# A loop that works out the order of the attention stage, and weights that load in halves

## The chip, the core and the metric

The kernel runs on one core of a Trainium2 chip. The core has five engines with a queue each: TensorE (PE, with its weight loads as PEld), VectorE (DVE), ScalarE (ACT), GpSimd (POOL) and SyncE (SP), which here only issues transfers. Each engine runs its queue in order. The metric is the time of one execution on the device in microseconds, the median of several runs.

## What is computed

Attention over 4 batches and 8 heads, 576 positions, head size 64, with a window of 128 and a slope per head; then a soft mixture of 8 experts on the 2304 rows of 512; then a layer with a squared ReLU.

```python
def _attn_ref(q, k, v):                      # (4, 8, 576, 64)
    scores = scale * q @ k.T
    scores = where((rel >= 0) & (rel < 128), scores + bias, -1e9)
    attn = exp(scores - max); attn /= sum(attn) + 1e-9
    return attn @ v
def _moe_ref(x, phi, w1, w2):                # x (2304, 512), 32 slots
    logits = x @ phi
    d = softmax(logits, axis=0)
    slot_input = (d.T @ x).reshape(8, 4, 512)
    slot_out[e] = maximum(slot_input[e] @ w1[e], 0) @ w2[e]
    return softmax(logits, axis=1) @ slot_out
def _moe2_ref(x, w_in, w_out):
    h = maximum(x @ w_in, 0)
    return h * h @ w_out
```

## The kernel before

The first stage, some 130 us, is attention with the dispatch half of the mixture. Its **units** are pairs of heads of one batch, 16 of them (u), four to a batch. A unit has 9 chunks of 64 rows (c); two chunks make a **step** (t), 72 steps. Of each step, in order of need:

- emit_S: two score products on TensorE (tile s, L166), into one of three PSUM banks "S".
- emit_max: on VectorE, bias added and the row's minimum taken (p, st, L174), into one of NP = 5 buffers p.
- emit_exp on ScalarE (L185), emit_sums on GpSimd (L190), emit_recip on VectorE (L195; for two steps together), emit_norm with emit_fold on GpSimd (L209, L219).
- emit_T: two transposes of p on TensorE (tile tp, L233). They free the buffer p for the step five later.
- emit_evac: the transposed blocks go to the ring ptb, first on ScalarE (L245), then the half blocks on VectorE (L249, L251).

When the steps of a unit are through, emit_PV (L261, tiles xa and xb) makes the product with v, emit_xT (L273, L278) copies it, and emit_xn transposes it back (X, L302; Y, L306) and copies it (xn_all, L307; xnr, L309). After four units come the logits (L, L289, L295) and then d0 to d4, the dispatch of that batch: max and exp of the logits, a transpose of dT (L339), its copy dn on VectorE (L340, L342), the product R with dn (L347, L350) and the sum acc (L357, L359).

**What sets the order.** The loop over t at L436 emits it by hand: scores of step t + 1, transposes of step t - LT (LT = 4), PV of a unit when its time has come, then evacuation, max, sums, exp, reciprocal and norm, and at last what run_side holds for that t (L390 to L419 fill the table). The order in which it is emitted is the order in each engine's queue.

**Transfers.** All go through SyncE's queue. When the scores of a unit's last chunk have been emitted, z and k of the unit two later (three later for the first two) are issued (L448 on; they wait until the buffer is free), and after them one weight tile of 1 MB, at units 4, 7, 10 and 13 two (load_next_w, L65). v of unit u + 2 follows emit_xT of unit u. The weight ring has 19 tiles. As the stage ends, pools close and five extra tiles and yw are loaded into their room. Then the products H (L650) and O (L789) use the weights.

Of the kernel before, what the change touches and what calls it, by code (L numbers as in the profile page):

```python
# [12 lines left out]
ALU = mybir.AluOpType  # L13
# [15 lines left out]
def attn_moe_relu2_kernel(ctx: ExitStack, tc: tile.TileContext, z, k, v, phi, w1, w2, w_in, w_out, bias, cst, out):  # L29
# [130 lines left out]
    def emit_S(t):  # L160
        sb_t[t] = bank("S", "s")
        if t % 2 == 0:
            st_t[t // 2] = apool.tile([128, 12], F32, tag="st", name="st", bufs=4)
# [5 lines left out]
    def emit_max(t):  # L169
        for i in range(2):  # L170
            u, c, n, e = info[2 * t + i]
            p = pbuf[t % NP][:, e:e + n]
            pr = u % NPAIR
            dve.tensor_tensor_reduce(  # L174
                out=p, in0=sb_t[t][:, 256 * i:256 * i + n], in1=tbl[:, 192 * pr + 192 - n:192 * pr + 192],
                scale=-0.125, scalar=3.0e38, op0=ALU.add, op1=ALU.min, accum_out=st_t[t // 2][:, 2 * (t % 2) + i:2 * (t % 2) + i + 1],
            )
        sb_t.pop(t)

    def emit_exp(t):  # L180
        st, k = st_t[t // 2], 2 * (t % 2)
        for i in range(2):
            u, c, n, e = info[2 * t + i]
            p = pbuf[t % NP][:, e:e + n]
            act.activation(out=p, in_=p, func=AF.Exp, bias=st[:, k + i:k + i + 1], scale=-1.0, accum_out=st[:, 4 + k + i:5 + k + i])  # L185
# [25 lines left out]
    def emit_norm(t):  # L211
        st, k = st_t[t // 2], 8 + 2 * (t % 2)
        emit_fold(t)
        for i in range(2):
            u, c, n, e = info[2 * t + i]
            o = e + n - 128 if c % 2 else e
            p = pbuf[t % NP][:, o:o + min(n, 128)]
            eng = dve if t >= NS - 2 and i == 1 else pool
            eng.tensor_scalar(out=p, in0=p, scalar1=st[:, k + i:k + i + 1], scalar2=0.0, op0=ALU.mult, op1=ALU.add)  # L219
# [52 lines left out]
    def emit_xT(u):  # L272
        act.activation(out=xT[u][:, 0:512], in_=xa_t.pop(u), func=AF.Copy)  # L273
        dst = xT[u][:, rem(u // NPAIR)]
# [7 lines left out]
    L_t = {}  # L282
# [14 lines left out]

    def emit_xn(u):
        kk = u % NPAIR
        X = bank("T" if kk == NPAIR - 1 or u == NU - 2 else "B", "X")  # L300
        for g in range(4):
            pe.transpose(X[:, 128 * g:128 * g + 128], xT[u][:, 128 * g:128 * g + 128], ident)  # L302
        sl = slice(128 * kk, 128 * kk + 128)
        if u // NPAIR % 2:
            Y = bank("T", "Y")
            pe.transpose(Y[:, 0:128], xT[u][:, 512:640], ident)  # L306
        dve.tensor_copy(out=xn_all[:, :, sl], in_=X.rearrange("p (g d) -> p g d", g=4))  # L307
        if u // NPAIR % 2:
            act.activation(out=xnr[:, sl], in_=Y[:, 0:128], func=AF.Copy)  # L309
# [26 lines left out]
    def emit_d2(b):  # L336
        X = bank("T", "X")
        for c in range(0, wid(b), 128):
            pe.transpose(X[:, c:c + 128], dT[:, c:c + 128], ident)  # L339
        dve.tensor_copy(out=dn[:, 0:128], in_=X[:, 0:128])  # L340
# [49 lines left out]
    side, side0 = {}, {}  # L390
    last_T = {}
    for u in range(NU):
        t0 = (NCH * u + 8) // 2 + (LT if u < NU - 1 else LT - 1)
        add = lambda dt, f, *a: side.setdefault(t0 + dt, []).append((f, a))
        side0.setdefault(t0 + 1, []).append((u,))
        add(1, emit_xT, u)
        late = u == NU - 1
        if late:
            break
        if u < NU - 2:  # L400
            add(4, emit_xn, u)
        if u % NPAIR == NPAIR - 1:
            for x in range(u - 3, u + 1):
                add(3, emit_logits, x)
            for x in range(u - 3, u + 1):
                add(3, emit_logr, x)
        if u == NU - 2:
            for x in range(u - 2, u + 1):
                add(3, emit_logits, x)
            for x in range(u - 2, u + 1):  # L410
                add(3, emit_logr, x)
        if u % NPAIR == NPAIR - 1:
            b = u // NPAIR
            add(4, emit_d0, b)
            add(5, emit_d1, b)
            add(6, emit_de, b)
            add(8, emit_d2, b)
            add(9, emit_d3, b)
            add(9, emit_d4, b)  # L419

    def run_side(t):
        for f, a in side.get(t, ()):
            f(*a)
            if f is emit_xT and a[0] + NQ < NU:
                load_v(a[0] + NQ)

    alone = (0, 1, NS - 2, NS - 1)
    T_at, sums_at = {}, {}
    for t in range(NS):
        T_at.setdefault(t + (LT - 1 if t in alone else LT), []).append(t)  # L430
        if t in alone:
            sums_at[t + 1] = (t, 1)
        elif t % 2:
            sums_at[t + 1] = (t - 1, 2)
    emit_S(0)
    for t in range(NS + LT):  # L436
        if t == LT - 1:
            emit_T(0)
            keep_warm("B", 2, idle)
        if t + 1 < NS:  # L440
            emit_S(t + 1)
            if t in (0, 2):
                keep_warm("B", 1, idle)
            for u, c, n, e in info[2 * t + 2:2 * t + 4]:
                if c == NCH - 1:
# [7 lines left out]
                    for _ in range(0 if u == 0 else 2 if u in (4, 7, 10, 13) else 1):  # L453
                        load_next_w()
        for x in T_at.get(t, ()):
            if x > 0:
                emit_T(x)
        for a in side0.get(t, ()):
            emit_PV(*a)
        for x in T_at.get(t, ()):  # L460
            emit_evac(x, 0)
        if t < NS:
            emit_max(t)
        done = sums_at.get(t, (0, 0))
        if done[1]:
            emit_sums(*done)
        if t < NS:
            emit_exp(t)
        if done[1]:
            emit_recip(*done)  # L470
        for x in range(done[0], done[0] + done[1]):
            emit_norm(x)
        for x in T_at.get(t, ()):
            emit_evac(x, 1)
        run_side(t)
        if t == NS - 2:
# [4 lines left out]
        if t == NS + LT - 2:  # L481
            pt.close()
            load_extra(1)
        if t == NS:
# [598 lines left out]
```

## Time and profile before

| | |
|---|---|
| median of 3 runs | 399.75 us (399.33 to 401.79) |
| the profiled execution | 402.85 us, span 401.1 us |
| PE, DVE, ACT, POOL busy | 96%, 70%, 61%, 29% of the span |
| transfers | 75.36 MB, mean 188 GB/s over the span |

The first stage ends at about 131 us, where the slices of the profile turn from attention to the H and O products; from 172 us on TensorE runs the last layer. The chain that ended last gives PE 81%, DVE 6% and DMA 5% of the span. In that chain s has 5%, xa 5%, the transfer of k 3% and tp 2%.

### The profile page before, as it was taken

The page shows a single profiled execution, that of the slowest core. Times are in us where ns is not written, and L with a number is a line of the kernel's source. Part 1 is how long each engine was busy: PE and PEld are TensorE (multiplying, and loading weights), DVE is VectorE, ACT ScalarE, POOL GpSimd, SP SyncE. Part 2 cuts the span into 40 slices and gives each one's busy share as a digit, 9 for nine tenths or more (in the row PEclk, how much of TensorE's full clock was granted, in tenths as well). Part 3 has the DMA queues.
Part 4 walks back from the last instruction along what each step waited for, and adds up shares of the span by engine and source line. Part 5 has one row for each costly group of instructions (what it writes and reads, how often), then busy time and mean ns, then how long its engine had stood idle before and what let it go on. Part 6 is the DMA issues. An engine that isn't in the chain of part 4 may idle for free.

```text
span 401.1 us, 7875 instructions
## 1 busy us (share of the span) xinstructions
PE 386.2 (96%) x2602; PEld 302.4 (75%) x2602; DVE 282.3 (70%) x861; ACT 245.0 (61%) x730; POOL 118.2 (29%) x290
## 2 busy tenths in 40 slices
PE   8899899999988999999999999999999999999995
PEld 8788777868865534687787888788877888888884
DVE  5687748768767685577867789786867774566454
ACT  5789858869876412178867765777667644433440
POOL 3877647766765041203111111111010000000000
PEclk9999989999999999999999999999999999999999
DMA  7979969999886999999602200000000040003004
GB/s 228 377 284 305 400 243 336 353 347 330 317 341 255 406 414 421 411 409 411 233 0 75 105 32 0 2 0 2 1 0 2 0 157 2 0 31 128 0 0 159
DMA packets 20489, 75.36 MB, mean 188 GB/s; under 512 B 2528, under 2 KB 4320, under 8 KB 16352
## 3 DMA queue, kind: packets, MB, share of 16 engines
q1 hardware_dynamic: 19872, 74.30, 48.8%
q10 hardware_dynamic: 576, 0.56, 0.5%
q8 instruction: 21, 0.34, 0.3%
q14 instruction: 20, 0.16, 0.1%
HBM read 70.13 MB, written 4.72 MB: 187 GB/s over the span
## 4 chain that ended last, share of the span: by engine, by line
PE 81%; DVE 6%; DMA 5%; ACT 3%; POOL 2%; issue 1%; SPq 0%; ACTq 0%; DVEq 0%; POOLq 0%
PE acc L886 48%; PE s L166 6%; PE xa L261 5%; PE h L842 4%; PE H L650 4%; PE O L789 4%; DMA kt<-in_k_dram 3%; PE tp L233 2%; DVE ptb L249 2%; DVE p L174 2%; DMA first<-in_k_dram 2%; POOL p L219 2%; PE L L289 1%; PE MX L738 1%; ACT p L185 1%
## 5 line engine op out<-in xcount | busy, mean ns | idle before, releaser
L886 PE MATMUL acc<-whl,arena_gh 128*128 128x512 f32 x864 | 216.4, 393 | 0.0
L886 PEld LDWEIGHTS acc<-whl,arena_gh 128*128 128x128 f32 x864 | 160.2, 188 | 35.2 <-issue 2.9
L871 DVE TENSOR_TENSOR arena_gh<-hT,arena_gh 128x384 fp32r<-128x384 f32 (+1 forms) x97 | 53.6, 553 | 30.1 <-ACT arena_gh L867 24.7
L185 ACT ACTIVATE p<-p,st 128x192 f32<-128x192 f32 (+1 forms) x144 | 61.4, 429 | 9.8 <-DVE st L174 8.0
L854 ACT ACTIVATE acc<-h 128x384 f32<-128x384 f32 x47 | 23.2, 493 | 64.9 <-PE h L842 64.9
L166 PE MATMUL s<-kt,zq 128*128 128x192 f32 (+2 forms) x270 | 55.3, 330 | 2.9 <-DMA kt<-in_k_dram 2.3
L698 POOL TENSOR_SCALAR yw<-f 128x512 f32<-128x512 f32 x32 | 27.1, 851 | 99.6 <-DVE arena_cin L715 49.3
L219 POOL TENSOR_SCALAR p<-p,st 128x128 f32<-128x128 f32 (+1 forms) x142 | 50.6, 371 | 8.8 <-DVE st L195 2.9
L249 DVE TENSOR_SCALAR ptb<-tp 64x128 f32<-64x128 f32 x112 | 31.9, 285 | 21.7 <-ACT ptb L245 19.7
L166 PEld LDWEIGHTS s<-kt,zq 128*128 128x128 f32 x270 | 42.2, 197 | 5.7 <-issue 2.4
L174 DVE CUSTOM_DVE_ANT_0 p<-s,tbl 128x192 f32<-128x192 f32 (+1 forms) x144 | 41.6, 325 | 2.9 <-PE s L166 2.5
L245 ACT ACTIVATE ptb<-tp 128x256 f32<-128x256 f32 (+1 forms) x72 | 25.0, 349 | 12.2 <-PE tp L233 11.5
L842 PE MATMUL h<-cst_sb,Mst 128*128 128x384 f32 x95 | 32.3, 339 | 0.1
L233 PE MATMUL tp<-cs,p 128*128 128x128 f32 x144 | 28.5, 277 | 2.1 <-POOL p L219 1.4
L209 POOL TENSOR_TENSOR p<-p 128x128 f32<-128x128 f32 (+1 forms) x64 | 27.1, 424 | 2.7
L261 PE MATMUL xa<-ptb,vt 128*64 128x256 f32 (+1 forms) x256 | 27.8, 359 | 0.0
L185 ACT ACTIVATION_READ_ACCUMULATOR p<-p,st 128x1 f32 x144 | 27.3, 190 | 0.0
L863 DVE TENSOR_TENSOR hT<-acc 128x384 f32<-128x384 f32 x17 | 9.5, 557 | 23.3 <-ACT acc L854 23.2
L867 ACT ACTIVATE arena_gh<-hT 128x384 fp32r<-128x384 f32 x48 | 24.8, 517 | 0.7
L867 ACT ACTIVATE arena_gh<-acc 128x384 fp32r<-128x384 f32 x47 | 24.2, 515 | 0.6
L261 PEld LDWEIGHTS xa<-ptb,vt 128*64 128x64 f32 x256 | 16.9, 136 | 9.4 <-issue 1.8
L233 PEld LDWEIGHTS tp<-cs,p 128*128 128x128 f32 x144 | 19.4, 143 | 5.8 <-POOL p L219 3.9
(204 smaller groups left out, 460.1 us busy)
## 6 DMA issues: line engine op xcount, KB each, us to landing
w_w<-in_w_dram SPq DMA_DIRECT2D x31, 1024.0 KB, 8.5
f<-in_w_in_dram SPq DMA_DIRECT2D x16, 512.0 KB, 10.2
f<-in_w_out_dram SPq DMA_DIRECT2D x16, 512.0 KB, 10.2
zq<-in_z_dram SPq DMA_DIRECT2D x13, 576.0 KB, 6.1
vt<-in_v_dram SPq DMA_DIRECT2D x16, 320.0 KB, 5.8
kt<-in_k_dram SPq DMA_DIRECT2D x13, 288.0 KB, 6.4
out_dram<-psum SPq DMA_DIRECT2D x11, 256.0 KB, 2.2
yw<-in_w_dram SPq DMA_DIRECT2D x1, 1024.0 KB, 10.1
```

The source lines that it names most:

```text
L166: pe.matmul(out=sb_t[t][:, 256 * i:256 * i + n], lhsT=zbuf(u)[:, c].rearrange("p a b -> p (a b)"), rhs=kt_t[u][:, 64 * c + 64 - n:64 * c + ...
L174: dve.tensor_tensor_reduce(out=p, in0=sb_t[t][:, 256 * i:256 * i + n], in1=tbl[:, 192 * pr + 192 - n:192 * pr + 192], scale=-0.125, scalar ...
L185: act.activation(out=p, in_=p, func=AF.Exp, bias=st[:, k + i:k + i + 1], scale=-1.0, accum_out=st[:, 4 + k + i:5 + k + i])
L209: pool.tensor_tensor(out=ap(True), in0=ap(True), in1=ap(False), op=ALU.subtract)
L219: eng.tensor_scalar(out=p, in0=p, scalar1=st[:, k + i:k + i + 1], scalar2=0.0, op0=ALU.mult, op1=ALU.add)
L233: pe.transpose(A[:, i, :], P[:, o:o + 128], ident)
L249: dve.tensor_scalar(out=dst, in0=src, scalar1=-1.0, scalar2=0.0, op0=ALU.mult, op1=ALU.max)
L261: pe.matmul(out=out, lhsT=v_t[u][:, j, po:po + 64], rhs=pt[:, a:b, po:po + 64], start=(j == 0 or (j == 3 and a == 2)), stop=(j == 4 or (j ...
L842: pe.matmul(out=hb[-1][:, 0:HB], lhsT=Mst[:, 128 * f:128 * f + 128], rhs=cst_sb[:, c0:c0 + HB], start=True, stop=True)
L867: act.activation(out=lo_t[i][1][hf][:, 0, cl], in_=rbuf[hf][:, cl], func=AF.Square)
L871: eng.tensor_tensor(out=gh[hf][:, 1, cl], in0=g[hf][:, cl], in1=gh[hf][:, 0, cl].bitcast(F32), op=ALU.subtract)
L886: pe.matmul(out=acc_t[s], lhsT=gh[:, x, c0:c0 + 128], rhs=w[:, f % 2, y, :], start=(units[i] in firsts and a == 0), stop=(units[i] in last ...
```

## The change

The work of the stage is now given as a list. Each operation has an engine, a listed duration in ns, the operations that it needs, a due time (STEP = 1450 ns per step) and the PSUM banks that it takes with the operations that free them. arrange() walks a clock for each of the four engines: it takes, again and again, the operation that can start first, and among equals the one due first. The order so found is emitted, one operation after the other, and so fixes each engine's queue. Transfers are not in the list; they are issued at the score steps as before.

Some functions are split so that their parts can move apart: emit_max, emit_exp and emit_norm by chunk, emit_fold from emit_norm, the copies of xT, xn, xnr and dn from what went before them.

A weight tile is loaded by two transfers of 512 KB (load_half_w); two are issued after each odd unit's last scores, three after each even one's and after unit 15's, 38 in all for the same 19 tiles.

```diff
+    half_w = []
+
+    def load_half_w():
+        if half_w:
+            t, src = half_w.pop()
+            sp.dma_start(out=t[:, 2:4], in_=src[:, 2:4])
+            return
+        key = wq.pop(0)
+        used[0] += 1
+        t = wt[key] = ring.tile([128, 4, 512], F32, tag="w", name=f"w_{key[0]}{key[1]}")
+        src = wsrc[key[0]][key[1]].rearrange("p (a b) -> p a b", a=4)
+        sp.dma_start(out=t[:, 0:2], in_=src[:, 0:2])
+        half_w.append((t, src))
...
+    def emit_max(t, i):
+        if t % 2 == 0 and i == 0:
+            st_t[t // 2] = apool.tile([128, 12], F32, tag="st", name="st", bufs=4)
...
+    ops, users = {}, {}
+
+    def op(f, arg, eng, ns, after=(), due=0, banks=(), lag=100):
+        ops[f, arg] = {"eng": eng, "ns": ns, "after": [x for x in after if x], "due": due, "banks": banks, "lag": lag}
+
+    def each(f, *args):
+        return [(f, a) for a in args]
+
+    STEP = 1450
...
+    for t in range(NS):
+        ch, t0 = info[2 * t:2 * t + 2], STEP * t
+        two = [(t, 0), (t, 1)]
+        steps = (t,) if t in alone else (t - 1, t) if t % 2 else (t, t + 1)
+        op(emit_S, t, "PE", sum(4 * n / 2.4 + 12 for u, c, n, e in ch), (), t0 - 1500, (("S", each(emit_max, *two)),), 170)
+        for i, (u, c, n, e) in enumerate(ch):
+            op(emit_max, (t, i), "DVE", n / 0.96 + 72, each(emit_S, t) + each(emit_T, *range(t - NP, t - NP + 1)[:t >= NP]), t0 + 100 * i, (), 140)
+            op(emit_exp, (t, i), "ACT", n / 1.4 + 303, each(emit_max, (t, i)), t0 + 400 + 100 * i)
+        if t == steps[0]:
+            op(emit_sums, (t, len(steps)), "POOL", 200, each(emit_exp, *[(x, i) for x in steps for i in range(2)]), STEP * steps[-1] + 1500)
+            op(emit_recip, (t, len(steps)), "DVE", 110, each(emit_sums, (t, len(steps))), STEP * steps[-1] + 1600)
+        whole = sum(x[2] == 192 for x in ch)
+        if whole:
+            op(emit_fold, t, "POOL", 182 + 138 * whole, each(emit_exp, *two), t0 + 1500)
+        for i, (u, c, n, e) in enumerate(ch):
+            eng = "DVE" if t >= NS - 2 and i == 1 else "POOL"
+            op(emit_norm, (t, i), eng, 345 if n > 64 else 290, each(emit_recip, (steps[0], len(steps))) + each(emit_fold, t)[:whole], t0 + 1900 + 100 * i, (), 70)
+        full = [(u, (c - 1) // 2) for u, c, n, e in ch if c]
+        half = [(u, c // 2 if c % 2 == 0 else c // 2 - 1) for u, c, n, e in ch if c != 1]
+        free = lambda l: each(emit_PV, *[owner[x] for x in l if owner[x] is not None])
+        op(emit_T, t, "PE", 222, each(emit_norm, *two), t0 + 3500, (("T", each(emit_evac, *two[:1 + bool(half)])),), 170)
+        op(emit_evac, (t, 0), "ACT", 80 + 100 * len(full), each(emit_T, t) + free(full), t0 + 4000)
+        if half:
+            op(emit_evac, (t, 1), "DVE", 208 * len(half), each(emit_T, t) + each(emit_evac, (t, 0)) + free(half), t0 + 4300)
...
+        op(emit_PV, u, "PE", 1840, each(emit_evac, *parts), t0 + 5500, (("xa", each(emit_xT, u)), ("T" if late else "B", each(emit_xTb, u))), 190)
...
+            op(emit_dn, b, "DVE", 320, each(emit_d2, b), t0 + 13500)
+            op(emit_d3, b, "PE", 1260 + 500 * odd, each(emit_dn, b) + each(emit_xn, *us) + each(emit_xr, *us) * odd, t0 + 14000, (("T", each(emit_d4, b)),), 190)
+            op(emit_d4, b, "DVE", 650 + 200 * (b > 0), each(emit_d3, b), t0 + 15000)
...
+    def arrange():
+        wait = {k: len(o["after"]) for k, o in ops.items()}
+        for k, o in ops.items():
+            for x in o["after"]:
+                users.setdefault(x, []).append(k)
+        ready, seen, order = dict.fromkeys(ops, 0), {}, []
+        clock = dict.fromkeys(("PE", "DVE", "ACT", "POOL"), 0)
+        held = {tag: [] for tag in NBUF}
+        can = {e: [k for k in ops if ops[k]["eng"] == e and not wait[k]] for e in clock}
+
+        def room(k):
+            when = 0
+            for tag, readers in ops[k]["banks"]:
+                if len(held[tag]) >= NBUF[tag]:
+                    for x in held[tag][len(held[tag]) - NBUF[tag]]:
+                        if x not in seen:
+                            return None
+                        when = max(when, seen[x])
+            return when
+
+        while len(order) < len(ops):
+            best = None
+            for e in clock:
+                for k in can[e]:
+                    r = room(k)
+                    if r is not None:
+                        x = (max(clock[e], ready[k], r), ops[k]["due"], len(order), k)
+                        if best is None or x[:2] < best[:2]:
+                            best = x
+            start, _, _, k = best
+            o = ops[k]
+            can[o["eng"]].remove(k)
+            clock[o["eng"]] = start + o["ns"]
+            seen[k] = start + o["ns"] + o["lag"]
+            for tag, readers in o["banks"]:
+                held[tag].append(readers)
+            for x in users.get(k, ()):
+                wait[x] -= 1
+                ready[x] = max(ready[x], seen[k])
+                if not wait[x]:
+                    can[ops[x]["eng"]].append(x)
+            order.append(k)
+        return order
...
-                    for _ in range(0 if u == 0 else 2 if u in (4, 7, 10, 13) else 1):
-                        load_next_w()
+                    for _ in range(0 if u == 0 else 3 if u % 2 == 0 or u == 15 else 2):
+                        load_half_w()
+        if f is emit_T and a == 0:
+            keep_warm("B", 2, idle)
+        if f is emit_xTb and a + NQ < NU:
+            load_v(a + NQ)
+
```

TensorE at the start of the stage (tile s, scores; tp, transposes; "first" holds z and k of unit 2, so its first rows are step 9; warm, matmuls on zeros). Before:

```order
L166 MATMUL s<-kt,zq_94 128x192 x4
L233 MATMUL tp<-cs,p_98 128x128 x2
L166 MATMUL s<-kt,zq_94 128x192 x2
L233 MATMUL tp<-cs,p_99 128x128 x2
L166 MATMUL s<-first 128x64
L166 MATMUL s<-first 128x128
L233 MATMUL tp<-cs,p_100 128x128 x2
L166 MATMUL s<-first 128x192 x2
L233 MATMUL tp<-cs,p_96 128x128 x2
L261 MATMUL xa<-ptb,vt 64x256 x6
```

And of the change:

```order
L178 MATMUL s<-kt,zq_94 128x192 x4
L242 MATMUL tp<-cs,p_97 128x128 x2
L178 MATMUL s<-kt,zq_94 128x192 x2
L178 MATMUL s<-first 128x64
L178 MATMUL s<-first 128x128
L242 MATMUL tp<-cs,p_98 128x128 x2
L242 MATMUL tp<-cs,p_99 128x128 x2
L178 MATMUL s<-first 128x192 x2
L242 MATMUL tp<-cs,p_100 128x128 x2
L178 MATMUL s<-first 128x192 x2
L242 MATMUL tp<-cs,p_96 128x128 x2
L178 MATMUL s<-first 128x192 x2
```

The transposes of steps 2 and 3 (p_98, p_99) moved behind the scores of step 9, and PV of unit 0 (xa) behind those of step 12.

SyncE's queue around z and k of unit 7 (zq_93 with the kt behind it). Before:

```order
L135 DMA zq_94<-in_z_dram 128x1152
L142 DMA kt<-in_k_dram 128x576
L70 DMA w_w_578<-in_w_dram 128x2048
L70 DMA w_w_580<-in_w_dram 128x2048
L146 DMA vt<-in_v_dram 128x640
L135 DMA zq_93<-in_z_dram 128x1152
L142 DMA kt<-in_k_dram 128x576
L70 DMA w_w_703<-in_w_dram 128x2048
```

And of the change:

```order
L149 DMA zq_94<-in_z_dram 128x1152
L156 DMA kt<-in_k_dram 128x576
L82 DMA w_w_470<-in_w_dram 128x1024
L88 DMA w_w_585<-in_w_dram 128x1024
L82 DMA w_w_585<-in_w_dram 128x1024
L160 DMA vt<-in_v_dram 128x640
L149 DMA zq_93<-in_z_dram 128x1152
L156 DMA kt<-in_k_dram 128x576
L88 DMA w_w_665<-in_w_dram 128x1024
L82 DMA w_w_665<-in_w_dram 128x1024
```

Three halves stand where two whole tiles stood ahead of unit 7's z and k, and two halves where one tile stood behind them.

VectorE at the dispatch of the second batch (ISA rows are emit_max, with their read-out; TENSOR_SCALAR is the evacuation; dn the copy that R needs). Before:

```order
L195 RECIPROCAL st<-st 128x4
L249 TENSOR_SCALAR ptb<-tp 64x128 x2
L174 ISA p_98,st<-s,tbl 128x192
L174 ISA st 128x1
L174 ISA p_98,st<-s,tbl 128x192
L174 ISA st 128x1
L249 TENSOR_SCALAR ptb<-tp 64x128 x2
L340 COPY dn<-X 128x128
L342 COPY dn<-X 128x32
```

And of the change:

```order
L206 RECIPROCAL st<-st 128x4
L359 COPY dn<-X 128x128
L361 COPY dn<-X 128x32
L187 ISA p_98,st<-s,tbl 128x192
L187 ISA st 128x1
L187 ISA p_98,st<-s,tbl 128x192
L187 ISA st 128x1
L258 TENSOR_SCALAR ptb<-tp 64x128 x4
```

The two copies dn moved ahead of a max step and the evacuations.

## Rows read from the trace of the kernel before

**Rows 1.** Busy time by stretch (us, instructions), granted clock, share and rate of transfers:

```profile
core 0: us, PE busy (x) PEld busy (x) DVE busy (x) ACT busy (x) POOL busy (x), PEclk, DMA share, GB/s
30.00:40.00 10.00, 9.93 (x104) 8.28 (x104) 7.42 (x45) 8.99 (x39) 7.71 (x22) 1.00 0.89 303
40.00:50.00 10.00, 8.44 (x105) 7.30 (x93) 7.71 (x45) 8.57 (x38) 6.85 (x21) 1.00 1.02 405
50.00:60.00 10.00, 9.43 (x67) 6.99 (x68) 4.97 (x26) 4.96 (x20) 4.71 (x14) 0.83 0.64 244
60.00:70.00 10.00, 9.96 (x84) 7.96 (x84) 8.46 (x45) 8.84 (x39) 7.35 (x22) 1.00 0.91 328
```

**Rows 2.** TensorE's waits up to 130 us: us in total, times, longest:

```profile
PE s L166 <- DMA kt<-in_k_dram: 2.3, 2, 2.1
PE tp L233 <- POOL p L219: 1.4, 2, 0.9
...
PE R L347 <- ACT p L185: 1.0, 1, 1.0
PE R L347 <- DVE dn L342: 0.9, 1, 0.9
```

**Rows 3.** Timeline of SyncE's queue, start and duration in us of each issue:

```profile
34.83 1.61 SPq L70 DMA_DIRECT2D w_w<-in_w_dram  x2
...
42.39 0.42 SPq L142 DMA_DIRECT2D kt<-in_k_dram  x1
...
133.28 0.44 SPq L529 DMA_DIRECT2D yw<-in_w_dram  x1
```

**Rows 4.** The k tiles, all instructions that touch kt:

```profile
DMA to landing us min/median/max: 2.9/5.6/8.0
```

**Rows 5.** Timeline of TensorE, the first scores of unit 7:

```profile
50.57 0.41 PE L166 MATMUL s<-kt,zq 128*128 128x64 f32 x2 [2.13 <-DMA kt<-in_k_dram]
```

**Rows 6.** Busy time by stretch, columns as in rows 1, 50 to 56 us:

```profile
50.00:52.00 2.00, 1.43 (x12) 0.58 (x12) 0.75 (x7) 0.77 (x4) 1.72 (x6) 0.84 0.86 315
52.00:54.00 2.00, 2.00 (x14) 1.16 (x7) 0.94 (x3) 0.49 (x3) 0.65 (x2) 0.50 1.06 421
54.00:56.00 2.00, 2.00 (x15) 1.59 (x16) 1.47 (x7) 0.96 (x5) 0.00 (x0) 0.81 0.69 286
```

**Rows 7.** Busy time by stretch, columns as in rows 1, behind the stage:

```profile
150.00:160.00 10.00, 10.00 (x135) 4.72 (x137) 5.93 (x14) 2.40 (x4) 2.03 (x2) 1.00 1.01 419
...
180.00:190.00 10.00, 10.00 (x53) 8.00 (x52) 7.86 (x14) 8.14 (x19) 3.97 (x6) 1.00 1.03 410
```

**Rows 8.** The page's transfers: times, KB each, median us from issue to landing:

```profile
yw<-in_w_dram SPq DMA_DIRECT2D x1, 1024.0 KB, 10.1
```

**Rows 9.** The H products with yw: duration in ns min/median/max, first and last start:

```profile
L650 PE MATMUL H<-yw,siT x8: 592/592/593, 145.3 to 145.8; 128*32 128x512 f32 x8
```

**Rows 10.** Timeline of all engines, the start of the stage:

```profile
13.04 0.38 PE L233 MATMUL tp<-cs,p 128*128 128x128 f32 x2
...
13.97 0.36 DVE L174 CUSTOM_DVE_ANT_0 p<-s,tbl 128x192 f32<-128x192 f32 x1
...
14.77 0.68 PE L166 MATMUL s<-first 128*128 128x64 f32 x4 [1.35 <-DMA first<-in_k_dram]
```

**Rows 11.** Timeline of all engines, the dispatch of the second batch:

```profile
82.95 0.17 DVE L342 COPY dn<-X 128x32 f32<-128x32 f32 x1
...
83.18 1.06 PE L347 MATMUL R<-xn_all,dn 128*32 128x512 f32 x8 [0.89 <-DVE dn L342]
```

**Rows 12.** Timeline of TensorE: two PV four units apart, and one gap between:

```profile
62.48 1.74 PE L261 MATMUL xa<-ptb,vt 128*64 128x256 f32 x16
...
75.35 0.61 PE L166 MATMUL s<-kt,zq 128*128 128x64 f32 x4
76.23 0.41 PE L233 MATMUL tp<-cs,p 128*128 128x128 f32 x2 [0.28 <-DVE ptb L249]
...
93.64 1.74 PE L261 MATMUL xa<-ptb,vt 128*64 128x256 f32 x16
```

**Rows 13.** The evacuations on VectorE: duration in ns min/median/max:

```profile
L249 DVE TENSOR_SCALAR ptb<-tp x112: 251/283/296, 11.0 to 129.0; 64x128 f32<-64x128 f32 x112
```

More of the change, by code (lines that the diff above doesn't have):

```diff
@@ L209, in emit_fold, with emit_norm @@
         pool.tensor_tensor(out=ap(True), in0=ap(True), in1=ap(False), op=ALU.subtract)
-    def emit_norm(t):
+    def emit_norm(t, i):
         st, k = st_t[t // 2], 8 + 2 * (t % 2)
[L213 to L219, printed above, removed]
+        u, c, n, e = info[2 * t + i]
+        o = e + n - 128 if c % 2 else e
+        p = pbuf[t % NP][:, o:o + min(n, 128)]
+        eng = dve if t >= NS - 2 and i == 1 else pool
+        eng.tensor_scalar(out=p, in0=p, scalar1=st[:, k + i:k + i + 1], scalar2=0.0, op0=ALU.mult, op1=ALU.add)
     def emit_T(t):
@@ L278, in emit_xT @@
             act.activation(out=dst, in_=xb_t.pop(u)[:, 0:64], func=AF.Copy)
-    L_t = {}
+    L_t, X_t, Y_t = {}, {}, {}
     def emit_logits(u):
@@ L296, in emit_logr, with emit_X, emit_Y, emit_xr @@
                       start=False, stop=(kk == 3), tile_position=(0, 32 * g), skip_group_check=True)
-    def emit_xn(u):
[L299 to L309, printed above, removed]
+    def emit_X(u):
+        kk = u % NPAIR
+        X_t[u] = bank("T" if kk == NPAIR - 1 or u == NU - 2 else "B", "X")
+        for g in range(4):
+            pe.transpose(X_t[u][:, 128 * g:128 * g + 128], xT[u][:, 128 * g:128 * g + 128], ident)
+    def emit_Y(u):
+        Y_t[u] = bank("T", "Y")
+        pe.transpose(Y_t[u][:, 0:128], xT[u][:, 512:640], ident)
+    def emit_xn(u):
+        sl = slice(128 * (u % NPAIR), 128 * (u % NPAIR) + 128)
+        dve.tensor_copy(out=xn_all[:, :, sl], in_=X_t.pop(u).rearrange("p (g d) -> p g d", g=4))
+    def emit_xr(u):
+        sl = slice(128 * (u % NPAIR), 128 * (u % NPAIR) + 128)
+        act.activation(out=xnr[:, sl], in_=Y_t.pop(u)[:, 0:128], func=AF.Copy)
     def emit_d0(b):
@@ new lines, in each @@
+    def each(f, *args):
+        return [(f, a) for a in args]
+    STEP = 1450
+    owner, last = {}, {}
+    for u in range(NU):
+        for j in range(5):
+            slot = jblk(u, j)
+            owner[u, j], last[slot] = last.get(slot), u
+    fin = {u: (NCH * u + NCH - 1) // 2 for u in range(NU)}
+    alone = (0, 1, NS - 2, NS - 1)
+    for t in range(NS):
[22 more added lines that the diff above has]
+            op(emit_evac, (t, 1), "DVE", 208 * len(half), each(emit_T, t) + each(emit_evac, (t, 0)) + free(half), t0 + 4300)
@@ L398, in attn_moe_relu2_kernel @@
         if late:
             break
+        x_all = each(emit_xT, u) + each(emit_xTb, u)
         if u < NU - 2:
[L401 to L442, printed above, removed]
+            tag = "T" if kk == NPAIR - 1 else "B"
+            op(emit_X, u, "PE", 436, x_all, t0 + 9000, ((tag, each(emit_xn, u)),), 170)
+            op(emit_xn, u, "DVE", 608, each(emit_X, u) + each(emit_d3, b - 1)[:b], t0 + 9500)
+            if odd:
+                op(emit_Y, u, "PE", 109, each(emit_X, u), t0 + 9010, (("T", each(emit_xr, u)),), 170)
+                op(emit_xr, u, "ACT", 175, each(emit_Y, u) + each(emit_d3, b - 1)[:b], t0 + 9500)
@@ L443, in attn_moe_relu2_kernel, with units_of, run @@
+    def units_of(b):
+        return range(NPAIR * b, NPAIR * b + (NPAIR if b < NB - 1 else NPAIR - 1))
+    def run(f, a):
+        if f in (emit_logits, emit_logr):
+            for u in units_of(a):
+                f(u)
+        else:
+            f(*(a if isinstance(a, tuple) else (a,)))
+        if f is emit_S:
+            if a in (1, 3):
                 keep_warm("B", 1, idle)
-            for u, c, n, e in info[2 * t + 2:2 * t + 4]:
+            for u, c, n, e in info[2 * a:2 * a + 2]:
@@ L452, in attn_moe_relu2_kernel @@
                         sp.dma_start(out=phi_sb, in_=phi)
-                    for _ in range(0 if u == 0 else 2 if u in (4, 7, 10, 13) else 1):
-                        load_next_w()
[L455 to L476, printed above, removed]
+                    for _ in range(0 if u == 0 else 3 if u % 2 == 0 or u == 15 else 2):
[4 more added lines that the diff above has]
+            load_v(a + NQ)
+    left = {f: sum(k[0] is f for k in ops) for f in (emit_S, emit_T, emit_norm)}
+    for f, a in arrange():
+        run(f, a)
+        if f not in left:
+            continue
+        left[f] -= 1
+        if left[f]:
+            continue
+        if f is emit_S:
             zt.close()
```

63 lines of the change are left out of this document (36 added, 27 removed).

## The prediction

> **What bounds the kernel now.** I began with the table of ten-microsecond stretches over the whole first stage, attention and its dispatch, which the change alone touches. TensorE is busy 9.93 and 9.96 of 10 us in two ordinary stretches, 30 to 40 and 60 to 70, while VectorE, ScalarE and GpSimd stand at 7.35 to 8.99 [rows 1]. So TensorE sets the pace there, and the reader should ask only what keeps it from issuing. Two stretches stand out: 40 to 50, where it was busy 8.44, and 50 to 60, where the granted clock was 0.83 [rows 1].
>
> The list of TensorE's waits up to 130 us names the reasons [rows 2]: 2.3 us for k tiles from memory, 1.0 and 0.9 us at the product R, and 1.4 us at two transposes in the drain. The ends of matmuls are modelled, so a wait shorter than the pipeline does not appear as idle. I therefore also read start-to-start distances in the timeline of TensorE.
>
> The k wait is the one of unit 7. Its transfer was issued at 42.39 [rows 3] and is the slowest of its kind, 8.0 us to landing where the median is 5.6 [rows 4]; two whole weight tiles had been issued 7.6 us before it, at 34.83 [rows 3]. The score matmul behind it stood 2.13 us [rows 5]. After that wait TensorE goes on at the lower of its two levels: the granted clock is 0.84, 0.50 (1.2 GHz) and 0.81 in three stretches of 2 us [rows 6]. That is (0.16 + 0.50 + 0.19) x 2 = 1.7 us of full-speed work, so the whole place costs 2.13 + 1.7 = 3.8 us.
>
> Behind the stage TensorE is busy 10.00 of 10 us while the transfers run full, at 410 to 419 GB/s [rows 7]. The nearest call is the tile yw: issued at 133.28 [rows 3], landed 10.1 us later [rows 8], at 143.4, and first used at 145.3 [rows 9]. So a stage that ends earlier passes its gain on, but with only 1.9 us to spare at yw.
>
> **The change part by part.** No matmul, activation or copy is added or removed; 38 transfers of 512 KB take the place of 19 of 1 MB. The rest is order. The planner runs when the program is built and costs the chip nothing.
>
> *Start.* The scores of step 9 need the first k of unit 2, and TensorE stood 1.35 us for it, until 14.77 [rows 10]. The planner knows nothing of transfers. Its order puts step 9 ahead of the transposes of steps 2 and 3, which stood before it; that of step 3 ran at 13.04 [rows 10]. They now leave after step 9, near 14.77 + 0.5 = 15.3. The max of a step reuses the buffer of the transpose five steps back, so the max of step 7, which ran at 13.97 [rows 10], has to wait for the transpose of step 2 and starts near 15.3 + 0.38 (its time in rows 10) + 0.1 = 15.8, 1.8 us later. Queued behind it on VectorE are the max of step 8 and, through the score banks, the scores of steps 10 and 11. Against that, PV of unit 0 now stands behind the scores of steps 11 and 12, work that is then already done. Bounds 0 and +1.8; I take half, +0.9, since the same work is only partly exchanged.
>
> *The k wait.* Before unit 7's k the queue now carries three halves in place of two tiles after the previous unit's z and k: 512 KB less, which at the 405 GB/s of 40 to 50 [rows 1] is 0.52 MB / 0.405 = 1.3 us earlier. The transfers were also not full in the stretch before, 303 GB/s from 30 to 40 [rows 1], and the halves of unit 2 now stand ahead of two v loads, so earlier bytes can fill that room. Further, the scores of step 31 now stand behind PV of unit 4 and two transposes, where scores and transposes alternated. Bounds 0 (it stays) and -3.8 (it goes, and the clock stays up). I take -3.8, because 1.3 us earlier and a need that comes one PV later (some 1.9 us) together exceed the 2.13 us.
>
> At this point the Trainium skill speaks against the change: its page DMA: Bandwidth & Descriptors, section Rules for kernel authors, asks for at least 1 MiB per DMA, and its Anatomy section fits 2.0 us fixed plus bytes over 436 GB/s for each transfer on the GpSimd path. By that fit 19 more transfers one after another would add 38 us to the queue, an estimate. The trace doesn't agree for a queue that is kept full.
>
> The rows: the 512 KB transfers of w_in and w_out ran at 410 GB/s from 180 to 190, the 1 MB ones at 419 from 150 to 160 [rows 7]; 19.9 MB at these rates differ by 1.0 us over the whole stage. I cost the size of the transfers at nothing; the cover is the tenth or so that the transfer engines have left in ordinary stretches (shares 0.89 and 0.91) [rows 1]. Each issue costs SyncE about 0.4 us [rows 3], and 19 more lie in its idle time.
>
> *R.* In the second batch R stood 0.89 us for dn, which was done at 82.95 + 0.17 [rows 11], and in the third 1.0 us [rows 2]. VectorE's order shows why: dn stood behind a max step and two evacuations. In the new order it stands ahead of them. TensorE's own work between the transposes of dT and R is about as long as before. R then starts about when TensorE reaches it: -1.9 for both, bounds 0 and -1.9.
>
> *Other gaps.* Over the four units between the PV at 62.48 and the one at 93.64 [rows 12] I compared each start-to-start distance with the shortest of its kind. Besides R there are four longer ones, about 1.1 us together; the largest is the 0.88 us at 75.35, with 0.28 of visible idle [rows 12]. For the 13 units between start and drain this makes 1.1 x 13 / 4 = 3.6 us. Bounds 0 and -3.6. I take half, -1.8: the planner looks at every engine's next free moment, which closes gaps of order, but its list books an evacuation on VectorE at 208 ns where the rows show a median of 283 [rows 13], which opens others.
>
> *Drain.* The chain of the last step (max, exp, reciprocal, norm, transpose, PV) is the same, with 1.4 us of idle in it [rows 2]. The copy xn_all (0.7 us) moves ahead of three max steps. Bounds -1.4 and +0.7; I take 0.
>
> *Fuller queue.* The same 39 MB now have to come in less time, and after the last scores three halves are queued where one tile was. That is 0.52 MB / 0.41 = 1.3 us later for the five extra tiles and yw, against 1.9 us to spare [rows 3, 8, 9]. Bounds 0 and 3.8 (one more k wait); I take +1.3.
>
> **Sum:** 0.9 - 3.8 - 1.9 - 1.8 + 0 + 1.3 = -5.3 us. The profiled execution took 402.85, and would take 397.55. It is 3.1 us above the median of the runs, 399.75, and above the slowest, 401.79. If the k wait is a part of what made it slow, the median has less of it to lose; I take the difference whole, 399.75 - 5.3 = 394.45, rounded to 394.4.
>
> **The rivals.**
> 1. *One k wait stays, at unit 7 or at another.* For it: the transfer engines are already busy 0.89 to 1.02 of the time in three of these stretches [rows 1], and the three halves come at even units, whose next issue is only four score steps away. Against it: the median k tile lands in 5.6 us [rows 4]. -5.3 + 3.8 gives 398.2. Chance 0.18.
> 2. *The order runs into several k waits*, the slower side. The place is the first score step of a unit; each costs 3.8, and transposes and PV stand queued behind it. At two the kernel is slower than before, -5.3 + 7.6 = +2.3, 402.0; at three, 405.8. It decides from two waits on. For it: the planner books no transfer at all. Against it: before, one place made up nearly all of TensorE's waits for k, 2.13 of 2.3 us [rows 2, 5]. Chance 0.12.
> 3. *VectorE runs behind the plan.* 75 ns on eight evacuations per unit, 16 units: 9.6 us of VectorE time. If half of that reaches TensorE, the gain is gone: 394.4 + 4.8 = 399.2. Against it: VectorE is busy 7.42 and 8.46 of 10 in the ordinary stretches [rows 1]. Chance 0.08.
> 4. *All gaps close*: -3.8 - 1.9 - 3.6 and the 1.4 of the drain, without the losses: -10.7, 389.0; with a part of it, up to 392. Chance 0.18.
> 5. *Halves are slow.* If a half held the queue as long as a tile, 38 x 2.5 us (1.05 MB at 419 GB/s) plus 47 us for z, k and v (16 units of 576 + 288 + 320 KB, 19.4 MB at 410 GB/s) make 142 us. Five extra tiles and yw behind them, 6 x 2.5 us, bring yw at 157, 12 us after its use at 145.3 [rows 9]: 394.4 + 12 = 406.4. Against it: rows 7. This is the rule of the Trainium skill named above. Chance 0.02.
>
> **How the numbers follow.** My forecast holds 0.42. About 1%, 4 us, is what a measurement of this kernel can tell from no change, so faster means under 395.75. The forecast lies near that edge: 0.32 of its 0.42 below it, with rival 4 in all 0.50. Same: 0.10 + 0.18 + 0.08 and the 0.02 of rival 2 that is two waits only, 0.38. Slower: 0.10 + 0.02 = 0.12. The range reaches from rival 4's lower end to beyond rivals 1 and 3, 389 to 401; it leaves out rivals 2 and 5 and the tail of 4, about 0.18. The likeliest case alone lies between 392.5 and 396.5.
>
> **What would show it.** In the changed profile: no k wait above 0.5 us and a granted clock of 1.00 between 40 and 60 (the term of 3.8); R's wait for dn gone in batches 2 and 3; the first PV behind the scores of step 12 and the second not more than 1 us later than before (start); the use of yw 5 us or more ahead of 145.3, with at most a short wait. The prediction is wrong if k waits appear at other units, if TensorE's gaps move to PV behind VectorE's evacuations, or if the stage ends earlier and H or O then wait for weights.

## Result and profile after

The change made the kernel slower: 404.48 us, the median of 4 runs (402.77 to 405.86), against 400.07 us of before; ratio of the runs 1.0089, interval 1.0060 to 1.0117, in which the quotient of the two medians, 1.0110, lies too. The prediction, 394.4 with a range of 389 to 401, was wrong in its sign.

TensorE's waits up to 130 us, after (us in total, times, longest):

```profile
PE xa L270 <- DMA vt<-in_v_dram: 2.8, 3, 1.6
PE tp L242 <- POOL p L228: 2.6, 4, 1.3
PE s L178 <- DMA first<-in_k_dram: 2.1, 1, 2.1
PE s L178 <- DVE st L187: 1.7, 3, 0.9
...
PE s L178 <- DMA kt<-in_k_dram: 0.2, 1, 0.2
```

Against [rows 2] the waits for k fell from 2.3 to 0.2 us and both waits of R are gone. In their place PV (xa) waits for v (vt), which it did not do before, the transposes tp wait longer for GpSimd, and the scores wait for VectorE. Busy time by stretch, columns as in [rows 1]:

```profile
30.00:40.00 10.00, 9.05 (x76) 7.87 (x75) 8.02 (x43) 8.74 (x36) 6.39 (x19) 1.00 0.72 234
40.00:50.00 10.00, 9.90 (x114) 8.01 (x114) 7.81 (x47) 8.15 (x36) 8.36 (x25) 1.00 0.97 362
50.00:60.00 10.00, 9.98 (x93) 7.30 (x92) 6.82 (x36) 7.76 (x33) 6.34 (x20) 1.00 0.86 309
60.00:70.00 10.00, 8.42 (x72) 7.51 (x73) 7.65 (x41) 7.74 (x34) 5.69 (x17) 1.00 0.92 335
```

From 40 to 60 TensorE now runs through, as forecast; 30 to 40 and 60 to 70, which were full, are not. From 30 to 40 it is one wait for VectorE:

```profile
32.60 0.92 PE L178 MATMUL s<-kt,zq 128*128 128x192 f32 x4 [0.95 <-DVE st L187]
```

The other places, one after the other. The start, all engines:

```profile
14.73 0.68 PE L178 MATMUL s<-first 128*128 128x64 f32 x4 [2.07 <-DMA first<-in_k_dram]
...
15.25 0.60 PE L242 MATMUL tp<-cs,p 128*128 128x128 f32 x4
...
15.67 0.36 DVE L187 CUSTOM_DVE_ANT_0 p<-s,tbl 128x192 f32<-128x192 f32 x1 [2.47 <-PE tp L242]
...
16.37 0.92 PE L178 MATMUL s<-first 128*128 128x192 f32 x4 [0.52 <-DVE st L187]
...
20.10 1.08 PE L270 MATMUL xa<-ptb,vt 128*64 128x256 f32 x8
```

While the transfer for step 9 is awaited, the transposes of steps 2 and 3 stand behind it, so VectorE stands 2.47 us as well and the max of step 7 runs at 15.67 instead of 13.97 [rows 10]. The first PV starts at 20.10, now with the scores of steps 11 and 12 ahead of it. SyncE's queue at unit 6, and the PV that waited:

```profile
52.88 0.33 SPq L149 DMA_DIRECT2D zq<-in_z_dram  x1
...
54.68 0.56 SPq L88 DMA_DIRECT2D w_w<-in_w_dram  x1
55.28 3.60 SPq L160 DMA_DIRECT2D vt<-in_v_dram  x2
```

```profile
63.73 1.73 PE L270 MATMUL xa<-ptb,vt 128*64 128x256 f32 x16 [1.58 <-DMA vt<-in_v_dram]
```

The v of unit 6 is issued at 55.28, behind z and k of unit 8 and three halves. R, which had waited 0.89 us [rows 11], runs without a wait:

```profile
83.84 1.06 PE L366 MATMUL R<-xn_all,dn 128*32 128x512 f32 x8
```

This profiled execution was the fastest of its kernel, and that of before (402.85) slower than the four others taken with it; of its 72 later runs one took longer (403.66). I therefore took both once more, below, and compare those.

### The profile page after: what moved, and what is told of

It is laid out like the page before. It is cut to its first block, busy times and chain, and to the rows that moved or that the text cites. A ratio compares the mean times of both kernels' runs of the same rounds, so it can differ in the third digit from the quotient of the medians.

```text
span 401.0 us, 7899 instructions
## 1 busy us (share of the span) xinstructions
PE 385.7 (96%) x2602; PEld 301.1 (75%) x2602; DVE 283.9 (71%) x861; ACT 245.8 (61%) x730; POOL 117.7 (29%) x290
## 4 chain that ended last, share of the span: by engine, by line
PE 80%; DMA 7%; DVE 6%; ACT 3%; SPq 1%; issue 1%; POOL 1%; ACTq 0%; DVEq 0%; POOLq 0%
PE acc L973 48%; PE s L178 6%; PE h L929 4%; PE xa L270 4%; DMA vt<-in_v_dram 4%; PE H L737 4%; PE O L876 4%; PE tp L242 2%; DVE ptb L258 2%; DMA first<-in_k_dram 2%; DVE p L187 1%; ACT p L196 1%; DMA kt<-in_k_dram 1%; PE L L300 1%; PE MX L825 1%
## 5 line engine op out<-in xcount | busy, mean ns | idle before, releaser
L178 PE MATMUL s<-kt,zq 128*128 128x192 f32 (+2 forms) x270 | 51.9, 326 | 1.1 <-DVE st L187 0.9
L242 PEld LDWEIGHTS tp<-cs,p 128*128 128x128 f32 x144 | 17.4, 141 | 8.5 <-POOL p L228 5.8
```

Of the source, the lines that this page charges most:

```text
L242: pe.transpose(A[:, i, :], P[:, o:o + 128], ident)
```

## Experiments

Ratios are against the kernel before, run in turns on the same chip, with 95% intervals. There were three groups, each on a chip of its own; the medians of before in them were 399.84, 400.51 and 399.71. Gains in us are against the change's first median, 404.48.

### The start

```diff
+        ready.update({(emit_S, t): 9000 for t in range(9, NS)})
```

> The arranged order with one fact more: in arrange(), scores from step 9 on are not ready before 9000 ns, which puts the scores of step 9 behind the transposes of steps 2 to 4, as before the change. Theory A (the start is lost because the loop knows of no transfer): PV of unit 0 comes back from 20.10 us to 16.5 to 17.5, PV of unit 3 from 39.9 to 36 to 37, and the time falls by 3 to 5 us from 404.5, to 399.5 to 401.5. Theory B (v queued late is what costs): the start is won but the v waits eat it, 403 to 404.5. Theory C (halves cost): no change beyond 1 us.

401.58 us, ratio 1.0045 (1.0024 to 1.0067): 2.9 us of the 4.4 came back. PV of unit 0 started at 17.60 and that of unit 3 at 37.38. All three lie just beyond what theory A had expected; it stands, with a rest: TensorE now stood 1.81 us at the transposes of step 4, which this edit had put ahead of the scores of step 9.

### v right behind PV

```diff
-        if f is emit_xTb and a + NQ < NU:
+        if f is emit_PV and a + NQ < NU:
```

> The arranged order with v of unit u + 2 issued right behind PV of unit u instead of behind the copy xTb. Theory B (v stands in SyncE's queue behind the next z, k and halves): the 2.8 us of TensorE's waits for vt fall under 0.5, the clock of the slower executions rises from 0.99 to 1.00, and the time falls by 2 to 3 us, to 401.5 to 402.5. Theory A (start): under 1 us of change. A loss would mean that the wait of the v issue for its buffer now holds up z and k behind it.

402.39 us, ratio 1.0057 (1.0032 to 1.0081). The waits for vt are gone from TensorE's list, and PV of unit 6 starts at 61.63 instead of 63.73. Theory B stands for 2.1 us; its further point, that the clock of the slower executions rises to 1.00, does not. Of its eight runs two had a clock of 0.999 (400.7 and 400.9 us), the others 0.992 to 0.995 (402.2 to 404.5), so the lower clock has another cause.

### Order alone, halves alone

The change with load_next_w and the counts of before; and the kernel before with load_half_w and the counts of the change:

```diff
-                    for _ in range(0 if u == 0 else 2 if u in (4, 7, 10, 13) else 1):
-                        load_next_w()
+                    for _ in range(0 if u == 0 else 3 if u % 2 == 0 or u == 15 else 2):
+                        load_half_w()
```

> The arranged order with whole weight tiles at the units of before: the order alone. Theory C (38 halves cost the queue): faster than 404.5 by 2 us or more. Theories A and B (the order is what costs): 403.5 to 405.5, and v waits as long or longer, since two whole tiles then stand ahead of some v.

> The kernel before with weights in halves at the counts of the change: the halves alone. Theory C: 2 us or more slower than 400.1. Theories A and B: within 1 us of 400.1. If the k wait of unit 7 that the profiled execution of before showed were in all its executions, and three halves in place of two tiles took it away, as the prediction has it, the time would fall by up to 3.8 us, to 396.3; if the k wait was of that execution alone, it stays at 400.

The order alone took 403.75 us, ratio 1.0100 (1.0067 to 1.0133), as slow as the change. One expectation failed: in its profiled execution TensorE waited for v 0.7 us, not 2.8 or more. So most of the wait for v needs the order and the halves together, yet without the halves the time is only 0.7 us less. The halves alone took 399.35, ratio 0.9982 (0.9969 to 0.9996): they win 0.5 us. So the order is the loss.

The halves alone also test the k wait. The scores of unit 7 waited for k no more, but R, which follows, did not come much earlier:

```profile
49.65 1.07 PE L361 MATMUL R<-xn_all,dn 128*32 128x512 f32 x8 [0.88 <-ACT p L199]
...
52.12 1.73 PE L275 MATMUL xa<-ptb,vt 128*64 128x256 f32 x16
```

In an ordinary execution of before (below), with 1.03 us of k wait, R starts at 49.81 and the PV behind it at 52.27. The copy dn that R needs runs at 49.23 here and at 49.27 there. So this k wait stood beside the wait for dn, and taking it away alone won 0.15 us. The 0.5 us of the halves do not lie in the stage at all: the last matmul of the kernel starts at 393.47, against 393.33, and what follows it is 0.7 us shorter (see the last section).

The Trainium skill's rule of at least 1 MiB per DMA (DMA: Bandwidth & Descriptors, Rules for kernel authors) was weighed in the prediction; here the measurement goes, by a little, the other way.

### The drain

```diff
-            op(emit_recip, (t, len(steps)), "DVE", 110, each(emit_sums, (t, len(steps))), STEP * steps[-1] + 1600)
+            op(emit_recip, (t, len(steps)), "DVE", 110, each(emit_sums, (t, len(steps))), STEP * steps[-1] + 1600 - (2500 if t >= NS - 4 else 0))
```

> The arranged order with the reciprocal of the last four steps due 2500 ns earlier, so that on VectorE it stands ahead of two evacuations instead of behind them; the norms of steps 68 to 71 and the last transposes hang on it. Theory D (the drain costs: one wait of 1.3 and one of 0.6 us close together at the last transposes, and in most executions a lower clock for some us after them, 0.77 and 0.81 in two stretches of 4 us, 1.7 us): PV of unit 15 comes 0.8 us earlier against that of unit 14's transposes, and 0.8 to 2.5 us are won, 402.0 to 403.7. Theory E (the drain is hidden by the transfers behind it): 404.5, since the H products then wait for weights.

401.99 us, ratio 1.0048 (1.0029 to 1.0066), 2.5 us won; in the same group the run of the listed time, below, took 404.83. TensorE at the end of the stage, of the change and of this run:

```profile
122.77 1.85 PE L270 MATMUL xa<-ptb,vt 128*64 128x256 f32 x16
...
127.04 0.44 PE L242 MATMUL tp<-cs,p 128*128 128x128 f32 x2 [1.33 <-POOL p L228]
128.06 0.41 PE L242 MATMUL tp<-cs,p 128*128 128x128 f32 x2 [0.58 <-POOL p L228]
...
129.53 1.73 PE L270 MATMUL xa<-ptb,vt 128*64 128x256 f32 x16
```

```profile
123.25 0.68 PE L242 MATMUL tp<-cs,p 128*128 128x128 f32 x2 [0.87 <-POOL p L228]
123.86 1.73 PE L270 MATMUL xa<-ptb,vt 128*64 128x256 f32 x16
...
126.92 0.44 PE L242 MATMUL tp<-cs,p 128*128 128x128 f32 x2 [0.50 <-POOL p L228]
...
128.41 1.73 PE L270 MATMUL xa<-ptb,vt 128*64 128x256 f32 x16
```

In the change the two waits stand close together, since a reciprocal that the last norms need stood behind two evacuations that were due earlier. Here one of them is split off ahead of the PV. Theory D stands, E falls.

### Start, v and drain together

> The arranged order with both edits, scores from step 9 on not before 9000 ns, and v issued right behind PV. If the two losses are separate, their gains add: 404.5 - 2.9 - 2.1 = 399.5 (398.5 to 400.5). If they are one and the same (a later start is what makes v late, or the transfers behind the stage take the gain back), it stays near 401.5.

> The arranged order with all three edits, start, v and drain. If the three are separate: 399.5 less 0.8 to 2.5, 397.0 to 398.7, below the kernel before (399.8) and below the halves alone (399.35). If the queue of transfers behind the stage is the next limit, no better than 399.3, with waits of the H products for weights.

401.12 us with two edits, ratio 1.0022 (0.9994 to 1.0049), and 400.19 with three, 0.9986 (0.9961 to 1.0011): less than the sum. The expected 399.5 and 397.0 to 398.7 were missed by 1.6 and 1.5 us. The profile of the first shows what stood in the way in that execution, in TensorE's timeline and in two stretches:

```profile
15.71 0.77 PE L242 MATMUL tp<-cs,p 128*128 128x128 f32 x2 [2.03 <-POOL p L228]
```

```profile
12.00:16.00 4.00, 1.97 (x14) 1.54 (x12) 3.19 (x17) 3.36 (x14) 2.39 (x9) 0.98 1.03 404
16.00:20.00 4.00, 4.00 (x18) 3.68 (x19) 2.34 (x15) 2.67 (x13) 2.94 (x9) 0.59 1.04 410
```

The rest that the start edit had left, a wait at the transposes of step 4, is followed by a stretch at a granted clock of 0.59: 0.41 x 4 = 1.6 us lost. The runs bear it out. Those with a mean clock of 0.999 or more, two of twelve with two edits and four of twelve with three, took 398.6 and 399.4, and 398.0 to 399.3, near the sums; the others were slower.

### The whole start, and two places exchanged

The start told in full, and the three edits with 8500 for 9000:

```diff
+        ready.update({(emit_S, t): (0 if t < 1 else 2500) if t < 9 else 11000 for t in range(NS)})
```

```diff
+        ready.update({(emit_S, t): 0 if t < 9 else 8500 for t in range(NS)})
```

> As with start, v and drain together, but the start told in full: scores of step 0 at 0, of steps 1 to 8 not before 2500 ns, from step 9 on not before 11000 ns. TensorE's order up to the scores of step 10 is then that of the kernel before (transposes of steps 2 and 3 ahead of step 9, that of step 4 behind it). If the 2.1 us by which PV of unit 0 still came late with the three edits (18.4 against 16.25 with the halves alone) and the lower clock after that wait are the rest of the loss: PV of unit 0 at 16 to 17, and the time 396.5 to 398.5, below every kernel so far. If the start's loss is given back later (the transfers set the end): 399.3 to 400.2, as with the three edits.

> As with start, v and drain together, with scores from step 9 on not before 8500 ns instead of 9000; in the start this changes the places of the scores of step 9 and the transposes of step 4 with each other. If TensorE's wait of 1.9 us at the transposes of step 4, with the scores of step 9 ready behind it, is the start's rest: 1 to 2 us faster than 400.2, 398.2 to 399.2. If not: 400.2 within 0.6.

The first took 399.76 us, ratio 0.9999 (0.9982 to 1.0017), a miss: PV of unit 0 came at 17.98, and the runs lay in two groups, at a clock of 0.999 to 1.000 (398.5 to 399.8) and at 0.994 to 0.998 (400.4 to 402.0). The second exchanges on TensorE nothing but the scores of step 9 and the transposes of step 4 (a few instructions of VectorE and GpSimd change places with it, between 16 and 20 us). It took 398.23, ratio 0.9956 (0.9942 to 0.9971): 2.0 us less than with 9000, and faster than the kernel before. All its 12 runs had a clock of 0.998 or more, between 397.7 and 399.4. Its start:

```profile
12.81 0.60 PE L242 MATMUL tp<-cs,p 128*128 128x128 f32 x4
14.77 0.68 PE L178 MATMUL s<-first 128*128 128x64 f32 x4 [1.35 <-DVE ptb L258]
15.44 0.62 PE L242 MATMUL tp<-cs,p 128*128 128x128 f32 x2
15.90 0.82 PE L178 MATMUL s<-first 128*128 128x192 f32 x4
...
17.52 1.73 PE L270 MATMUL xa<-ptb,vt 128*64 128x256 f32 x16
```

The wait of 1.35 us is put down to VectorE here, but it ends at 14.77, as in [rows 10], where the transfer was named.

### The listed time of an evacuation

```diff
-            op(emit_evac, (t, 1), "DVE", 208 * len(half), each(emit_T, t) + each(emit_evac, (t, 0)) + free(half), t0 + 4300)
+            op(emit_evac, (t, 1), "DVE", 285 * len(half), each(emit_T, t) + each(emit_evac, (t, 0)) + free(half), t0 + 4300)
```

> The arranged order with the evacuation on VectorE listed at 285 ns instead of 208, as the rows show it (251 to 296). Rival 3 of the prediction (VectorE runs behind the plan): 1 to 4 us faster, 400.5 to 403.5. Theories A, B and D (start, v and drain): 404 to 405, within 0.7 us of the change, since none of the three places is mended by it.

404.83 us, ratio 1.0114 (1.0085 to 1.0142). A truer number in the list changed TensorE's order in many places (PV of unit 2 came at 31.48 instead of 33.45), but not the time. So rival 3, in the form tested, that the wrong number is what costs, is not borne out.

### Both kernels once more

> The kernel before once more, for another profiled execution. If the k wait of unit 7 with the lower clock behind it (3.8 us in the prediction) is in ordinary executions: 2 us of wait at the scores of unit 7 and a granted clock near 0.5 for some us behind it, at 400 us. If it was of one execution alone: under 0.7 us of wait there, no lower clock, PV of unit 15 near 126 instead of 129.0, at 399 to 400.5.

> The changed kernel once more, for another profiled execution; the first was the fastest of four, with a mean clock of 0.999, the other three had 0.99. If the rest of the loss is the lower clock behind TensorE's waits: 404 to 406 us, and two stretches of some 4 us at a clock near 0.5 to 0.8, behind the start (16 to 20 us) or the drain (124 to 132 us). If the clock falls somewhere else or nowhere, the waits are not what sets it.

Before: 399.91 us, near its median. TensorE's waits for k, its timeline at unit 7's scores, and the stretches behind:

```profile
PE s L166 <- DMA kt<-in_k_dram: 1.8, 3, 1.0
```

```profile
49.24 0.41 PE L166 MATMUL s<-kt,zq 128*128 128x64 f32 x2 [1.03 <-DMA kt<-in_k_dram]
```

```profile
50.00:52.00 2.00, 2.00 (x18) 1.18 (x11) 1.82 (x7) 1.44 (x6) 1.80 (x5) 1.00 0.99 385
52.00:54.00 2.00, 2.00 (x25) 1.40 (x25) 1.59 (x11) 1.10 (x5) 0.79 (x4) 1.00 1.06 427
```

A wait of 1.03 us, between the two expectations, and no lower clock, where [rows 5, 6] had 2.13 and 1.7; the last PV came at 126.06, as expected for the case that it was of one execution. After: 404.42 us, its median too. Its waits, and the two places where its clock fell:

```profile
PE xa L270 <- DMA vt<-in_v_dram: 2.8, 3, 1.1
PE tp L242 <- POOL p L228: 2.4, 3, 1.3
...
PE s L178 <- DMA kt<-in_k_dram: 0.6, 2, 0.4
```

```profile
12.00:16.00 4.00, 2.16 (x16) 1.66 (x14) 1.99 (x12) 2.12 (x9) 1.41 (x5) 0.96 1.03 407
16.00:20.00 4.00, 4.00 (x16) 3.42 (x16) 3.18 (x18) 3.35 (x15) 3.70 (x11) 0.61 1.04 407
...
128.00:132.00 4.00, 3.91 (x40) 2.88 (x42) 1.71 (x6) 0.38 (x1) 0.92 (x2) 0.57 0.56 217
```

Behind the start it lost (0.04 + 0.39) x 4 = 1.7 us, behind the drain 0.43 x 4 = 1.7 us. The first, second, second to last and last PV, of before and of after:

```profile
16.25 1.74 PE L261 MATMUL xa<-ptb,vt 128*64 128x256 f32 x16
...
22.01 1.73 PE L261 MATMUL xa<-ptb,vt 128*64 128x256 f32 x16
...
120.81 1.73 PE L261 MATMUL xa<-ptb,vt 128*64 128x256 f32 x16
...
126.06 1.73 PE L261 MATMUL xa<-ptb,vt 128*64 128x256 f32 x16
```

```profile
20.16 1.73 PE L270 MATMUL xa<-ptb,vt 128*64 128x256 f32 x16
...
24.64 1.74 PE L270 MATMUL xa<-ptb,vt 128*64 128x256 f32 x16
...
122.82 1.85 PE L270 MATMUL xa<-ptb,vt 128*64 128x256 f32 x16
...
130.56 1.65 PE L270 MATMUL xa<-ptb,vt 128*64 128x256 f32 x8
```

After is 3.9 us late at the first, 2.6 at the second, 2.0 at the second to last and 4.5 at the last. A PV is a fair mark only where TensorE has the same work behind it. At the first it has not: after has issued 52 matmuls of scores, before 44, the two steps that now stand ahead of it. At the second both have issued 60, and 20 transposes. At the second to last after lacks the two transposes of one step, 0.2 us, so it is 2.2 us late in work; at the last both are level again. While the last PV runs, the lower clock goes on; from the first H product (140.58 against 135.51) to the last matmul (398.41 against 393.33) after is 5.1 us late. Behind the last matmul it gets 0.7 back, which leaves 4.4; the times differ by 404.42 - 399.91 = 4.5 us.

So the order loses 2.6 us at the start and 5.1 - 2.2 = 2.9 in the drain, wins 0.4 between them, and 0.7 come back at the very end.

## Why the prediction was wrong, step by step

- **Start, +0.9: mis-sized, measured +2.6.** The mechanism was right: the max of step 7 was forecast for 15.8 and ran at 15.67. The exchange that the prediction set against it was there too: the first PV is 3.9 us late, the second, at equal work, 24.64 - 22.01 = 2.6, so 1.3 us were work done ahead. The step that failed is "Bounds 0 and +1.8", of which half was then taken: 1.8 was the delay of one instruction, not of what hangs on it. Three further gaps, 0.52, 0.27 and 0.20 us at the next scores and transposes, followed in the first execution. In the second the transfer landed 0.5 us earlier and the lower clock took 1.7 us; its second PV was no later for it (24.64 against 24.57). With the experiment on the start alone 2.9 us came back; with step 9 in its old place, and v and drain mended, the second PV came at 22.76.
- **The k wait, -3.8: the wait did go, but was not worth that.** It was read from one execution, 402.85 us, that lay above the four runs taken with it and above all but one of the 72 later ones. An ordinary one has 1.03 us at this place and full clock; the waits for kt fell from 1.8 to 0.6 us, worth 1.2. The prediction saw the 3.1 us between profile and median, and still took the difference whole; that sentence is the failing step. 3.8 of the 5.3 us forecast stood on it. Its reason, bytes that come earlier, held for the wait and not for the time: the halves alone took this wait away and won 0.15 us, since R waited for dn beside it. The gain came with the new order, in which R finds dn ready; that TensorE also reaches this place later, when k is there, these runs do not tell apart from it.
- **R, -1.9: right.** 0.89 and 0.96 us in the ordinary execution of before, none after.
- **Other gaps, -1.8: mis-sized, about nothing.** From the second to the second to last PV the change wins 0.4 us of equal work. That is 1.2 of k and 1.9 of R, less 2.8 of v, and leaves 0.1 for all else. It is a remainder, not measured by itself. Gaps opened where others closed: 0.46 us at 27.00, at transposes that waited for GpSimd, and 0.95 us at 32.60 in the first execution of after.
- **Drain, 0: wrong, +2.9.** The chain was the same, but the order on VectorE put one reciprocal of it behind two evacuations. In the first execution, at full clock, the first H product was 138.99 - 135.51 = 3.5 us late, in the second 5.1; the 1.6 us between them are clock, and 1.3 are the order. The bound of +0.7 looked only at the copy xn_all. The edit of the reciprocal alone won 2.5 us.
- **v, not in the sum: +2.8.** The diff showed load_v hung on emit_xTb, a copy that the loop may place late. Only the queue around z and k of unit 7 was looked at, where v stands where it stood. At unit 6 it went behind five transfers. The experiment won 2.1 us.
- **Fuller queue, +1.3: not seen.** What the stage loses or wins goes through to the last matmul one to one: after is 5.1 us late at the first H product and at the last matmul. With step 9 in its old place both come 1.3 and 1.2 us earlier than before.
- **Size of the transfers, 0: right** for the stage, and 0.5 to 0.7 us are won behind the last matmul; rival 5 falls. Rival 2 gave nearly the time that came, 402 to 405.8, but by another transfer: k waits shrank, v waits came. That its number fits is luck.

Of the signs that the prediction named, two came true (no k wait above 0.5 us and full clock from 40 to 60; no wait at R) and two did not (the second PV within 1 us; yw needed 5 us earlier). None of the three by which it would have called itself wrong appeared: no k wait above 0.5 us at another unit, no PV behind VectorE's evacuations, no H or O product that waited for weights. It looked for its error at the wrong transfer. The sum of what was found, 2.6 - 1.2 - 1.9 - 0.1 + 2.8 + 2.9 - 0.7 = 4.4 us, closes on the 4.5 because the gaps are its remainder.

## What to carry to other kernels

A loop that orders work by listed times orders well only what is in its list: here it won 3.1 us (R and k) and lost 8.3 (start, drain and v), and one release time, one trigger and one due date turned it from 404.5 to 398.2 us. The release time had to be found: with v and drain mended, 9000 ns gave 400.2, the start told in full 399.8 and 8500 ns 398.2. When a change turns a hand order into a planned one, follow each queue that the plan does not know, and read the first and last batch by themselves. A wait that is to pay for a forecast must be in an execution whose time is that of the median, and must not stand beside another wait that ends as late. To say how late a changed order is, compare it where both orders have done the same work.

## What the hardware showed that was not expected

TensorE's clock set much of the spread between executions of the same kernel. It fell to the lower level for part of a stretch of some 4 us behind waits of TensorE that were 1.3 to 2.0 us long and had shorter ones near them (granted 0.57 to 0.61), for 1.6 to 1.7 us each time, and in the first execution of before behind one of 2.13 us [rows 5, 6]. In the first execution of after the start's wait was 2.07 us, and the clock stayed at 1.00; so it did behind 1.58 us for the same transfer in the second execution of before. Why it falls in one execution and not in the next isn't settled by these runs. What they show is that the last kernel, without the wait of 1.9 us at step 4, had a clock of 0.998 or more in all its runs, and that 1.3 us of wait, with 0.6 close behind, were followed by 1.7 us of lost clock in one drain and by none in another.

The end of the kernel is the other surprise. From the start of the last matmul to the end of the span the eleven profiled executions with weights in halves took 4.11 to 4.15 us, the three with whole tiles 4.73 to 4.98, though the code there is the same and the halves had been loaded more than 200 us before. In the halves alone the last stores landed sooner, the last at 3.3 us behind the start of that matmul instead of 3.8. Why is open.
